# Attention, then a squared-ReLU MLP, on one core: the last norms spread over units, one batch's split operands spread over items, and another order of the second product

## The chip, the cores and the metric

The kernel runs on one core of one Trainium2 chip (trn2). The metric is the device time of one execution in microseconds (us); the time before is the median of three runs. The engines are called PE (TensorE, matmuls), DVE (VectorE), ACT (ScalarE), POOL (GpSimd) and SP (SyncE, which issues the DMAs).

## The reference

Shapes: batch B = 4, heads H = 8, sequence S = 576, head dimension D = 64; the MLP has 2304 tokens, model width 512 and inner width 2048.

```python
scores = q @ k.T / sqrt(D)
x = (log1p(|i - j|) / log1p(max(i, 1)))[..., None]
scores = scores + (relu(x @ w1 + b1) @ w2).transpose(2, 0, 1)[None]
attn = exp(scores - max(scores)); attn = attn / (sum(attn) + 1e-9)
x = (attn @ v).transpose(0, 2, 1, 3).reshape(B * S, H * D)
out = relu(x @ w_in) ** 2 @ w_out
```

## The kernel before, in words

**Attention.** The work is a list of units `(b, hp, ic)`: batch, pair of heads, and one of five chunks of 128 query rows (the fifth, `ic == TAIL`, has 64 rows of both heads). The first NA = 40 units belong to batches 0 and 1 and run chunk by chunk, so that the bias table can be built beside them; the others belong to batches 2 and 3 and run pair of heads by pair of heads. A unit u has on PE: the scores (`score_products`, L429, into `sp`, four PSUM banks), two units later the transposes of the exponentials (`transposes`, L509 into banks a and b as `pp`, L512 into bank c as `pa`), and three units later the product with v (`values`, L528, bank d as `px`). TL = 2 is that distance. DVE adds the bias and finds the row maximum (L439), ACT takes the exponential (L444), which also sums the rows, and copies the transposes to SBUF (L778 in phase one, L963 in phase two).

**Norms.** When a pair of heads has all its chunks, its sums are inverted (`norm_inverse`, DVE, L454), split into three bf16 parts (`norm_parts`, POOL, L460), turned round by one matmul (`norm_rows`, L467, tile `rp`), copied by ACT (`norm_copy`, L472, tile `rows`), spread over the partitions by ten small matmuls (`spread_rows`, L489, tiles `ra` and `rt` in banks a and b), and multiplied into the result `xT` by DVE (`times_rows`, L495). In phase two, `norm_job` queues these steps as stages of a job. Each stage names its engine, a cost and, as the last entry, the first unit in which it may run.

**Order in phase two.** In each step s of the loop at L949 the program writes the order out: scores of s, transposes of s - 2, then for each of two halves ACT's copies and the exponential, between them the values of s - 3 and `fill(s, 0)`; then `fill(s, 1)` and `fill(s, 2)`. `fill(s, slot)` goes through the waiting jobs and issues each first stage whose slot this is, whose unit has come and for whose engine there is room. `SLOT` puts PE and ROW stages into slot 0, LAST (the multiplies) into 2 and all others into 1; `lag` says whether the next stage of a job may run in the same step. Before, `rp` of a norm stands in slot 0 of step u + 3 at the end of PE's unit, its copy `rows` right behind it, and the spreading in slot 0 of step u + 4. Units 37, 38 and 39 are those of phase one whose norms fall into phase two.

**MLP.** The weights and x are split into a high and a low part, and the first product uses seven products of sums and differences of blocks in place of eight. 40 items `(n, P)` (n: 512 tokens of batch n, or for n = B the four rests of 64; P: one of eight pairs of inner blocks) are processed in the order of `runs`; items 0 to 3 are of batch 0, items 4 to 7 of batch 1. Iteration i of the loop at L1135 has on PE the first products of item i (`products`, L1027, into `ha` and `hb`, 24 and 18 matmuls) and then the second product of item i - 1 (`down`, L1119, into four banks y0 to y3, 24 matmuls, or 12 for n = B). Between them other engines do, in program order: the parts `gh` (ACT, L1063) and `gl` (DVE, L1064) of item i - 1; `lead` of raw weight tiles (ACT L186, DVE L188 to L192), ACT's copy of their high part (L644) and POOL's low part (L650); the combinations `c` of item i (ACT L1041, DVE L1043 to L1046); `sums_x`, `high_x`, `low_x` (POOL L719, ACT L725, DVE L732), which make the seven operands m = 1 to 7 of a later batch at the items in `split_at`; and the squared ReLU of item i (ACT L1052 and L1053 for the first 32 items). `leave` takes finished banks y to SBUF (ACT copies, or DVE adds at L1089 where part of the sum was stored before) and issues the DMA.

The second product was, for each half f of the item and each bank k:

```python
for m, (a, x) in enumerate(((gh, wh), (gh, wl), (gl, wh))):
    PE.matmul(y_t[n][k], lhsT=a[:, slot, o:o + 128], rhs=x, ...)
```

The PSUM banks a to d of the attention become y0 to y3 of the MLP, in the order in which the y tiles are first made.

Of the kernel before, what the change touches and what calls it, by code (L numbers as in the profile page):

```python
# [68 lines left out]
TL = 2  # L69
# [8 lines left out]
def attention_then_relu2_mlp(ctx: ExitStack, tc: tile.TileContext, q, k, v, cols, w_in, w_out, psi, xmat, dist, out):  # L78
# [378 lines left out]
    def norm_parts(s):  # L457
        parts = att.tile([128, 3, 9], BF16, name="parts", tag="parts", bufs=2)
        for n in range(3):
            POOL.tensor_copy(out=parts[:, n], in_=s)  # L460
            if n < 2:
                POOL.tensor_tensor(out=s, in0=s, in1=parts[:, n], op=ALU.subtract)
        return parts

    def norm_rows(parts, tag=None):
        rp = bank("rp", tag)[:27, :128]
        PE.matmul(rp, lhsT=parts.rearrange("p n c -> p (n c)"), rhs=ident_b, start=True, stop=True)  # L467
        return rp

    def norm_copy(rp):  # L470
        rows_t = att.tile([27, 128], BF16, name="rows", tag="rows", bufs=2)
        ACT.copy(rows_t, rp)  # L472
        return rows_t
# [162 lines left out]
    def lead(n, upto=7):  # L636
        if upto & 1:
            scratch[n] = stage_p["p"].tile([128, 2, 256], F32, name="wa", tag="wa", bufs=3)
        lead_w(n, scratch[n].bitcast(I32), upto)
# [70 lines left out]
    def halves(n, m):  # L710
        one, op, two = RIGHT[m]
        for cs, *half in x_pieces(n):
            yield cs, op, half[one[1]][:, 2 * one[0]:2 * one[0] + 2], half[two[1]][:, 2 * two[0]:2 * two[0] + 2] if op else None

    def sums_x(n, ms):
        for m in ms:
            for cs, op, a, b in halves(n, m):
                if op:
                    POOL.tensor_tensor(out=sum_at[m][:, :, cs], in0=a, in1=b, op=op)  # L719

    def high_x(n, ms):
        for m in ms:
            hi = split_to[n % 2][m][0]
            for cs, op, a, b in halves(n, m):
                ACT.activation(out=hi[:, :, cs], in_=sum_at[m][:, :, cs] if op else a, func=AF.Identity, scale=xsig[n])  # L725

    def low_x(n, ms):
        w = width[n]
        for m in ms:
            hi, lo = split_to[n % 2][m]  # L730
            for cs, op, a, b in halves(n, m):
                DVE.scalar_tensor_tensor(out=lo[:, :, cs], in0=sum_at[m][:, :, cs] if op else a, scalar=xsig[n], in1=hi[:, :, cs], op0=ALU.mult, op1=ALU.subtract)  # L732
            xs_t[n, m] = (hi[:, :, :w], lo[:, :, :w])

    def store_x(n):
# [63 lines left out]
    room = {}  # L799

    def lag(a, b):
        return int(a != b and a != "PE" and (a, b) != ("DVE", "POOL"))

    SLOT = {"PE": 0, "ROW": 0, "LAST": 2}

    def job(at, *stages):
        jobs.append([at, list(stages)])
# [18 lines left out]
    def norm_job(u):  # L826
        b, hp, ic = units[u]
        st = {"s": sum_t.pop((b, hp))}
        job(
            u + 1,  # L830
            ("DVE", 0.4, lambda: norm_inverse(st["s"])),
            ("POOL", 1.3, lambda: st.update(parts=norm_parts(st["s"])), u + TL),
            ("PE", 0, lambda: st.update(rp=norm_rows(st["parts"], "a")), u + TL + 1),
            ("ROW", 0.24, lambda: st.update(rows=norm_copy(st["rp"]))),
            ("PE", 0, lambda: st.update(r=spread_rows(st["rows"], ("a", "b"))), u + TL + 2),
            ("LAST", 0.9, lambda: times_rows(b, hp, *st["r"])),
        )
        jobs.insert(len(norms), jobs.pop())
        norms.append(jobs[len(norms)])
# [103 lines left out]
    with tc.manual_schedule():  # L943
        job(NA + 1, *(("DVE", 0.68, lambda k=k: scan(k)) for k in range(NF)))
        x_job(NA + 4, 0)
        x_job(NA + 7, 1)
        for u in range(NA - TL - 1, NA):
            norm_job(u)
        for s in range(NA, NU + TL + 2):  # L949
            now[0] = s  # L950
            full = s < NU and units[s][2] < TAIL
            room["DVE"] = min(room.get("DVE", 0), 0.3) + (1.65 if full else 2.5)
            room["ACT"] = min(room.get("ACT", 0) + (0.45 if full else 1.9), 1.5)
            loads(s)
            if s == NA:
                for m, tag in enumerate(raws):
                    fetch_in(ins[m], tag)
            if s < NU:
                negm, sps = score_products(s, False)
            copies = transposes(s - TL, ("a", "b", "c")) if s - TL < NU else []  # L960
            for n in range(2):
                for c in copies[n:n + 1 if n == 0 else None]:
                    ACT.copy(*c)  # L963
                if n:
                    px = values(s - TL - 1, "d") if s - TL - 1 < NU else None
                    fill(s, 0)
                if s < NU and n < len(sps):
                    softmax(s, n, negm, sps[n])
            while waiting:
                b, hp, rows_t = waiting.pop(0)  # L970
                times_rows(b, hp, *spread_rows(rows_t, ("a", "b")))
            if s < NU and ends(s):
                norm_job(s)
            fill(s, 1)
            fill(s, 2)
            if px:
                keep_values(s - TL - 1, *px)
# [19 lines left out]
    lead_at = {1: (6, 7), 2: (10, 11), 3: (14,), 4: (15,)}  # L997
    lead_at.update({5: (16,), 9: (17,), 12: (20,), 13: (21,), 14: (18, 19), 15: (22, 23)})
    lead_at.update(zip(range(18, 26), ((n,) for n in range(24, 32))))
    split_at = {0: (1, (2, 5, 3, 4)), 3: (1, (1, 6, 7))}  # L1000
    split_at.update({i + j: (n, ms) for i, n in ((6, 2), (10, 3), (30, B)) for j, ms in enumerate(((2, 5, 3, 4), (1, 6, 7)))})
    largest_at = {4: 2, 8: 3, 28: B}
    raw_outs = [18, 19, 22, 23, 26, 27, 30, 31]
# [27 lines left out]
    def sums(i, ha, hb):  # L1031
        n, P = items[i]
        w = width[n]
        alpha = alpha_t[n]
        if i % 2:
            c, s = (take(1, o, 1024).rearrange("p (m t) -> p m t", m=4)[:, :, :w] for o in (4480, 5504))
        elif i < NP // 2:
            c, s = (tmp_p.tile([128, 4, 256], F32, name=x, tag=x) for x in "cs")
        else:
            c, s = (xT[1][:, :, 256 * x:256 * x + w] for x in range(2))  # L1040
        ACT.activation(out=s, in_=ha[:, :, :w], func=AF.Identity, scale=alpha)  # L1041
        stt = DVE.scalar_tensor_tensor
        stt(out=c[:, 2:4], in0=ha[:, 1:3, :w], scalar=alpha, in1=s[:, 0:4:3], op0=ALU.mult, op1=ALU.subtract)  # L1043
        stt(out=c[:, 0:2], in0=ha[:, 2:4, :w], scalar=alpha, in1=s[:, 0:2], op0=ALU.mult, op1=ALU.add)
        stt(out=c[:, 2:4], in0=hb[:, 0:1, :w].to_broadcast([128, 2, w]), scalar=alpha, in1=c[:, 2:4], op0=ALU.mult, op1=ALU.add)  # L1045
        stt(out=c[:, 2:4], in0=hb[:, 1:3, :w], scalar=alpha, in1=c[:, 2:4], op0=ALU.mult, op1=ALU.add)  # L1046
        c_t[i] = c

    def squares(i):
        c = c_t[i]  # L1050
# [6 lines left out]
    def parts_g(i):  # L1057
        c, w = c_t[i], width[items[i][0]]
        for f in range(2):
            gh = mlp.tile([128, 2, 256], F32R, name="gh", tag="gh", bufs=2)[:, :, :w]  # L1060
            gl = mlp.tile([128, 2, 256], F32R, name="gl", tag="gl", bufs=2)[:, :, :w]
            g = c[:, 1 - f:4:2]
            ACT.copy(gh, g)  # L1063
            DVE.tensor_tensor(out=gl, in0=g, in1=gh.bitcast(F32), op=ALU.subtract)  # L1064
            g_t[i, f] = (gh, gl)
# [38 lines left out]
    def down(i):  # L1104
        n, P = items[i]
        w = width[n]
        nk = w // 64
        if (n, P) in firsts:
            y_t[n] = [py_p.tile([128, 512], F32, name=f"y{k}") for k in range(nk)]
        order = [(f, k) for f in range(2) for k in range(nk)]  # L1110
        if i == NI - 1:
            order.sort(key=lambda x: x[1])
        for f, k in order:
            wh, wl = w_t[4 * P + 2 + f]
            gh, gl = g_t[i, f]
            t, o = divmod(128 * k, w)
            slot = t if f else 1 - t
            for m, (a, x) in enumerate(((gh, wh), (gh, wl), (gl, wh))):
                PE.matmul(  # L1119
                    y_t[n][k], lhsT=a[:, slot, o:o + 128], rhs=x,  # L1120
                    start=((n, P) in firsts and f == 0 and m == 0), stop=((n, P) in lasts and f == 1 and m == 2),
                )
            if (n, P) in lasts and f == 1:
                leave(n, P, k)
        if (n, P) in lasts and P < NP - 1:
            for j in range(2):
                part_y[n, j] = ready_y[j, "dram"]

    tmp_p = tmp_stack.enter_context(tc.tile_pool(name="tmp", bufs=1, side="right", reuse_waits="tile"))
    with tc.manual_schedule():  # L1130
# [4 lines left out]
        for i in range(NI + 1):  # L1135
# [11 lines left out]
            if i:  # L1147
                parts_g(i - 1)
            one, *two = lead_at.get(i, (None,))
            if one is not None:  # L1150
                lead(one)
            if i < NI:
                sums(i, ha, hb)
# [18 lines left out]
                fetch_out(raw_outs.pop(0))  # L1172
            if i in split_at:
                low_x(*split_at[i])
            if i + 1 in split_at:
                sums_x(*split_at[i + 1])
            if i in largest_at:
# [63 lines left out]
```

## Time and profile before

| what | value |
|---|---|
| median of 3 runs | 747.92 us (747.54 to 748.41) |
| profiled execution, its own time | 748.49 us |
| its span | 746.7 us |
| PE busy | 712.3 us (95%) |
| DVE busy | 556.7 us (75%) |
| ACT busy | 473.8 us (63%) |
| POOL busy | 180.0 us (24%) |
| mean granted clock of PE | 0.971 |

A row of a timeline is one stretch of like instructions of one engine: start, length, line, output<-inputs, shape, count, and in brackets the idle time before it and what ended that. The granted clock (PEclk) is a share of full speed. PE's matmuls overlap a little in these rows, so durations in the prediction are taken from start to start.

### The profile page before, as it was taken

What the parts mean: (1) busy time and instruction counts of PE and PEld (TensorE: products, weight loads), DVE (VectorE), ACT (ScalarE), POOL (GpSimd) and SP (SyncE); (2) the same over time, 40 slices, a digit from 0 to 9 for tenths busy, and PEclk for the clock granted to TensorE, in tenths of its full rate; (3) what the DMA queues carried; (4) which work ended last, traced back from release to release, by engine and by line L of the source; (5) the groups of instructions that cost most, each with busy time, mean ns of one, the idle gap of its engine ahead of it and who ended that gap; (6) DMA issues with size and microseconds to landing.
All of it is one profiled execution on the core that took longest, in us unless ns stands there. A gap on an engine that the chain in (4) does not pass through costs nothing. (4 is left out here: it accounts for less than half of the span.)

```text
span 746.7 us, 18201 instructions
## 1 busy us (share of the span) xinstructions
PE 712.3 (95%) x7382; PEld 576.5 (77%) x7382; DVE 556.7 (75%) x1186; ACT 473.8 (63%) x946; POOL 180.0 (24%) x289
## 2 busy tenths in 40 slices
PE   6889999999989999999998999999999999999992
PEld 6867878787767776777786888888888888888881
DVE  6699888885667889888898878878568775567661
ACT  4367887877756878888756756776476564455220
POOL 1464333332110037432442213112011112001000
PEclk7599999999999999999999999999999999999997
DMA  6630000003437512410442241240038322533100
GB/s 203 192 92 19 3 18 2 2 2 92 174 114 255 185 48 84 136 57 3 142 183 99 109 188 65 105 188 26 1 114 312 124 72 99 212 114 113 57 2 29
DMA packets 31608, 75.34 MB, mean 101 GB/s; under 512 B 5540, under 2 KB 13732, under 8 KB 30500
## 3 DMA queue, kind: packets, MB, share of 16 engines
q1 hardware_dynamic: 31524, 74.17, 28.7%
q8 instruction: 58, 0.95, 0.5%
q14 instruction: 26, 0.21, 0.1%
HBM read 55.81 MB, written 18.35 MB: 99 GB/s over the span
## 5 line engine op out<-in xcount | busy, mean ns | idle before, releaser
L1119 PE MATMUL y<-w,gh 128*128 128x512 f32 x576 | 182.9, 399 | 2.4 <-ACT gh L1063 1.5
L1027 PEld LDWEIGHTS <-area 128*128 128x128 f16 x1680 | 147.6, 98 | 24.8 <-issue 10.1
L439 DVE CUSTOM_DVE_ANT_0 t<-sp,area 128x576 f32<-128x576 f32 x144 | 103.7, 753 | 32.5 <-PE sp L429 29.9
L1119 PEld LDWEIGHTS y<-w,gh 128*128 128x128 f32 x576 | 105.9, 189 | 24.2 <-ACT gh L1063 3.2
L444 ACT ACTIVATE p<-t,negm 128x576 f32<-128x576 f32 x144 | 111.5, 776 | 13.2 <-DVE negm L439 13.0
L1119 PE MATMUL y<-w,gl 128*128 128x512 f32 x288 | 113.8, 395 | 0.7 <-DVE gl L1064 0.7
L429 PE MATMUL sp<-k,q 64*128 64x288 f32 (+1 forms) x640 | 99.6, 426 | 1.6 <-DMA q<-in_q 1.2
L528 PE MATMUL px<-pt,v 128*64 128x128 f32 (+1 forms) x1600 | 97.6, 269 | 2.3 <-DVE bt L384 1.2
L528 PEld LDWEIGHTS px<-pt,v 128*64 128x64 f32 x1600 | 79.9, 138 | 17.7 <-issue 5.9
L1027 PE MATMUL ha<-area 128*128 128x256 f16 (+1 forms) x816 | 85.4, 260 | 0.0
L509 PE MATMUL pp<-ident,p 128*128 128x128 f32 x576 | 83.0, 282 | 0.4 <-DVE xT L495 0.3
L509 PEld LDWEIGHTS pp<-ident,p 128*128 128x128 f32 x576 | 62.1, 141 | 22.7 <-issue 9.3
L389 POOL TENSOR_TENSOR area<-bt,bt 128x256 f32<-128x256 f32 x72 | 53.7, 768 | 73.6 <-DVE bt L384 73.6
L429 PEld LDWEIGHTS sp<-k,q 64*128 64x128 f32 (+1 forms) x640 | 52.7, 175 | 22.6 <-issue 8.0
L367 DVE TENSOR_TENSOR mask<-sdist,theta 128x1024 f16<-128x1024 f16 x81 | 56.1, 728 | 13.8 <-PE bb L397 7.6
L1119 PEld LDWEIGHTS y<-w,gl 128*128 128x128 f32 x288 | 54.4, 189 | 14.1 <-DVE gl L1064 2.0
L1027 PE MATMUL hb<-area 128*128 128x256 f16 (+1 forms) x612 | 64.9, 260 | 0.0
L963 ACT COPY pt<-pp 128x512 f32<-128x512 f32 x76 | 43.8, 577 | 30.0 <-PE pp L509 30.0
L1064 DVE TENSOR_TENSOR gl<-area,gh 128x512 fp32r<-128x512 f32 (+1 forms) x40 | 25.8, 668 | 29.7 <-ACT gh L1063 28.1
L778 ACT COPY pt<-pp 128x512 f32<-128x512 f32 x68 | 37.6, 587 | 14.1 <-PE pp L509 14.0
L650 POOL TENSOR_TENSOR w<-wa,w 128x512 fp32r<-128x512 f32 x16 | 20.8, 1299 | 86.6 <-ACT w L644 86.6
L1064 DVE TENSOR_TENSOR gl<-xT,gh 128x512 fp32r<-128x512 f32 (+1 forms) x36 | 25.6, 749 | 20.8 <-ACT gh L1063 19.2
(161 smaller groups left out, 1042.9 us busy)
## 6 DMA issues: line engine op xcount, KB each, us to landing
raw<-in_w_in SPq DMA_DIRECT2D x32, 512.0 KB, 4.1
r<-in_w_out SPq DMA_DIRECT2D x16, 512.0 KB, 5.0
xs<-area SPq DMA_DIRECT2D x4, 1792.0 KB, 13.3
py<-o SPq DMA_DIRECT2D x12, 512.0 KB, 3.4
o<-py SPq DMA_DIRECT2D x12, 512.0 KB, 4.1
v<-in_v SPq DMA_DIRECT2D x16, 320.0 KB, 4.1
q<-in_q SPq DMA_DIRECT2D x32, 128.0 KB, 3.0
out<-o SPq DMA_DIRECT2D x8, 512.0 KB, 2.9
```

What stands on the lines that cost most here:

```text
L367: DVE.tensor_tensor(out=out, in0=win, in1=th, op=ALU.is_ge)
L389: POOL.tensor_tensor(out=dst, in0=tw, in1=sw, op=ALU.add)
L429: mm = PE.matmul(out_t[to, x, :HALF], lhsT=qt[rows, cols], rhs=kt[rows, k0:k0 + HALF], start=True, stop=True)
L439: DVE.tensor_tensor_reduce(out=t.rearrange("p (x n) -> p x n", x=2), in0=sp[:, :, :HALF], in1=bias.rearrange("p (x n) -> p x n", x=2), sca ...
L444: ACT.activation(out=p[:, S * n:S * n + S], in_=t, func=AF.Exp, bias=negm[:, n:n + 1], scale=-1.0, accum_out=sums[:, 2 * ic + n:2 * ic + n ...
L509: PE.transpose(pp[:, 128 * c:128 * c + 128], p[:, k0:k0 + 128], ident)
L528: PE.matmul(px[64 * h:64 * h + 64, :w], lhsT=vt[:, c, h], rhs=src, start=(c == 0), stop=(c == 4))
L778: ACT.copy(dst, src)
L963: ACT.copy(*c)
L1027: PE.matmul(h[:, s, :w], lhsT=a, rhs=x, start=(k == 0), stop=(k == 5))
L1064: DVE.tensor_tensor(out=gl, in0=g, in1=gh.bitcast(F32), op=ALU.subtract)
L1119: PE.matmul(y_t[n][k], lhsT=a[:, slot, o:o + 128], rhs=x, start=((n, P) in firsts and f == 0 and m == 0), stop=((n, P) in lasts and f == 1 ...
```

## The change

At the boundary one norm goes to each of the steps 42, 43 and 44; in all norms of phase two `rp` moves to a new slot 3 behind the scores, into bank c, with its copy at once. The operands m = 1, 6, 7 of batch 1 are made one per item in items 1, 2 and 3 (all three were made in item 3), their sums in the used scratch tile `s` of the item before; the lead of weight tile 15 moves from item 4 to the end of item 3. The banks of y are made in the order 2, 3, 0, 1, and in each half of `down` all products with gh come ahead of those with gl.

```diff
+    def sum_of(n, m):
+        return sum_at.get((n, m), sum_at.get(m))
...
-                    POOL.tensor_tensor(out=sum_at[m][:, :, cs], in0=a, in1=b, op=op)
+                    POOL.tensor_tensor(out=sum_of(n, m)[:, :, cs], in0=a, in1=b, op=op)
...
     def lag(a, b):
-        return int(a != b and a != "PE" and (a, b) != ("DVE", "POOL"))
+        return int(a != b and a not in ("PE", "ROW") and (a, b) != ("DVE", "POOL"))
 
-    SLOT = {"PE": 0, "ROW": 0, "LAST": 2}
+    SLOT = {"PE": 0, "ROW": 3, "LAST": 2}
...
             ("DVE", 0.4, lambda: norm_inverse(st["s"])),
-            ("POOL", 1.3, lambda: st.update(parts=norm_parts(st["s"])), u + TL),
-            ("PE", 0, lambda: st.update(rp=norm_rows(st["parts"], "a")), u + TL + 1),
-            ("ROW", 0.24, lambda: st.update(rows=norm_copy(st["rp"]))),
-            ("PE", 0, lambda: st.update(r=spread_rows(st["rows"], ("a", "b"))), u + TL + 2),
+            ("POOL", 1.3, lambda: st.update(parts=norm_parts(st["s"])), u + TL + (u < NA)),
+            ("ROW", 0.24, lambda: st.update(rows=norm_copy(norm_rows(st["parts"], "c"))), u + TL + 2 + (u < NA)),
+            ("PE", 0, lambda: st.update(r=spread_rows(st["rows"], ("a", "b"))), u + TL + 2 + (u < NA)),
             ("LAST", 0.9, lambda: times_rows(b, hp, *st["r"])),
...
                 negm, sps = score_products(s, False)
+            fill(s, 3)
             copies = transposes(s - TL, ("a", "b", "c")) if s - TL < NU else []
...
-    split_at = {0: (1, (2, 5, 3, 4)), 3: (1, (1, 6, 7))}
+    split_at = {0: (1, (2, 5, 3, 4)), 1: (1, (1,)), 2: (1, (6,)), 3: (1, (7,))}
+    ahead = {3: 15}
...
         c_t[i] = c
+        if i + 1 in split_at and i < NP // 2 - 1:
+            n, (m,) = split_at[i + 1]
+            sum_at[n, m] = s[:, 0:2]
...
+            gl = mlp.tile([128, 2, 256], F32R, name="gl", tag="gl", bufs=2)[:, :, :w]
             gh = mlp.tile([128, 2, 256], F32R, name="gh", tag="gh", bufs=2)[:, :, :w]
-            gl = mlp.tile([128, 2, 256], F32R, name="gl", tag="gl", bufs=2)[:, :, :w]
...
-            y_t[n] = [py_p.tile([128, 512], F32, name=f"y{k}") for k in range(nk)]
-        order = [(f, k) for f in range(2) for k in range(nk)]
+            banks = {k: py_p.tile([128, 512], F32, name=f"y{k}") for k in (2, 3, 0, 1) if k < nk}
+            y_t[n] = [banks[k] for k in range(nk)]
+        order = [(f, k, m) for f in range(2) for ms in ((0, 1), (2,)) for k in range(nk) for m in ms]
...
-            if one is not None:
+            if one is not None and one not in ahead.values():
                 lead(one)
...
                 low_x(*split_at[i])
+            if i in ahead:
+                lead(ahead[i])
             if i + 1 in split_at:
                 sums_x(*split_at[i + 1])
```

## Rows read from the trace of the kernel before

**Rows 1.** The page, busy us (share of the span) and instructions, PE alone.

```profile
PE 712.3 (95%) x7382; PEld 576.5 (77%) x7382; DVE 556.7 (75%) x1186; ACT 473.8 (63%) x946; POOL 180.0 (24%) x289
```

**Rows 2.** The chain of waits: start us, us, what; two stretches of the second product.

```profile
395.67 6.79 PE y L1119 x22
...
427.59 5.48 PE y L1119 x24
```

**Rows 3.** Stretches of 2 us: busy us (instructions) of the engines, PEclk, DMA share, GB/s.

```profile
222.00:224.00 2.00, 2.00 (x15) 1.67 (x15) 1.51 (x5) 1.71 (x4) 0.00 (x0) 0.50 0.00 0
396.00:398.00 2.00, 2.00 (x6) 1.52 (x6) 1.90 (x5) 0.32 (x1) 0.00 (x0) 0.50 0.00 0
```

**Rows 4.** Timeline of PE at the boundary, start us, us, line, tiles [idle before].

```profile
213.85 0.22 PE L467 MATMUL rp<-ident_b,parts 128*27 128x128 bf16 x1 [0.56 <-POOL sums L462]
...
215.16 1.10 PE L509 MATMUL pp<-ident,p 128*128 128x128 f32 x8
...
217.54 0.41 PE L489 MATMUL ra<-rows,pick 27*64 27x128 bf16 x8
...
218.73 0.41 PE L489 MATMUL ra<-rows,pick 27*64 27x128 bf16 x8 [0.73 <-DVE xT L495]
...
219.92 0.22 PE L467 MATMUL rp<-ident_b,parts 128*27 128x128 bf16 x1 [0.75 <-DVE xT L495]
...
221.24 1.87 PE L509 MATMUL pp<-ident,p 128*128 128x128 f32 x8
...
225.23 0.41 PE L489 MATMUL ra<-rows,pick 27*64 27x128 bf16 x8
```

**Rows 5.** Tile rt, 230 to 360 us, idle before its instructions until (us, times).

```profile
  ACT pt L963: 1.5, 4
```

**Rows 6.** Timeline of PE at the start of the MLP.

```profile
371.79 0.70 PE L1119 MATMUL y<-w,gh 128*128 128x512 f32 x2 [0.85 <-DVE xT L495]
...
377.66 2.79 PE L1027 MATMUL ha<-area 128*128 128x256 f16 x24
...
382.18 0.71 PE L1119 MATMUL y<-w,gh 128*128 128x512 f32 x2
...
394.29 0.73 PE L1119 MATMUL y<-w,gh 128*128 128x512 f32 x2 [1.54 <-ACT gh L1063]
395.67 0.80 PE L1119 MATMUL y<-w,gl 128*128 128x512 f32 x1 [0.65 <-DVE gl L1064]
...
402.30 2.79 PE L1027 MATMUL ha<-area 128*128 128x256 f16 x24
```

**Rows 7.** Timeline of DVE at the start of the MLP.

```profile
377.91 0.42 DVE L188 TENSOR_SCALAR wa<-wa 128x512 f32<-128x512 f32 x1
...
381.44 1.95 DVE L1064 TENSOR_TENSOR gl<-area,gh 128x512 fp32r<-128x512 f32 x2 [1.20 <-ACT gh L1063]
...
385.57 0.74 DVE L1043 SCALAR_TENSOR_TENSOR c<-ha,small,s 128x512 f32<-128x512 f32 x1
...
388.33 0.92 DVE L188 TENSOR_SCALAR wa<-wa 128x512 f32<-128x512 f32 x1
...
401.15 0.74 DVE L732 SCALAR_TENSOR_TENSOR area<-area,small 128x512 f16<-128x512 f32 x1
```

**Rows 8.** Timeline of POOL at the start of the MLP.

```profile
376.00 1.30 POOL L650 TENSOR_TENSOR w<-wa,w 128x512 fp32r<-128x512 f32 x1 [10.54 <-ACT w L644]
...
387.68 1.29 POOL L719 TENSOR_TENSOR area<-xT 128x512 f32<-128x512 f32 x1
```

**Rows 9.** Timeline of ACT at the start of the MLP.

```profile
380.27 0.62 ACT L644 CAST w<-wa 128x512 fp32r<-128x512 f32 x1
380.80 1.13 ACT L1063 CAST gh<-area 128x512 fp32r<-128x512 f32 x2
...
399.08 0.72 ACT L725 ACTIVATE area<-area,small 128x512 f16<-128x512 f32 x1
```

**Rows 10.** Timeline of DVE at the end of a later run of items.

```profile
572.72 2.73 DVE L1089 TENSOR_TENSOR o<-o,y 128x512 f32<-128x512 f32 x4 [1.36 <-PE y L1119]
```

More of the change, by code (lines that the diff above doesn't have):

```diff
@@ L724, in high_x @@
             for cs, op, a, b in halves(n, m):
-                ACT.activation(out=hi[:, :, cs], in_=sum_at[m][:, :, cs] if op else a, func=AF.Identity, scale=xsig[n])
+                ACT.activation(out=hi[:, :, cs], in_=sum_of(n, m)[:, :, cs] if op else a, func=AF.Identity, scale=xsig[n])
     def low_x(n, ms):
@@ L731, in low_x @@
             for cs, op, a, b in halves(n, m):
-                DVE.scalar_tensor_tensor(out=lo[:, :, cs], in0=sum_at[m][:, :, cs] if op else a, scalar=xsig[n], in1=hi[:, :, cs], op0=ALU.mult, op1=ALU.subtract)
+                DVE.scalar_tensor_tensor(out=lo[:, :, cs], in0=sum_of(n, m)[:, :, cs] if op else a, scalar=xsig[n], in1=hi[:, :, cs], op0=ALU.mult, op1=ALU.subtract)
             xs_t[n, m] = (hi[:, :, :w], lo[:, :, :w])
@@ L1108, in down @@
         if (n, P) in firsts:
-            y_t[n] = [py_p.tile([128, 512], F32, name=f"y{k}") for k in range(nk)]
-        order = [(f, k) for f in range(2) for k in range(nk)]
+            banks = {k: py_p.tile([128, 512], F32, name=f"y{k}") for k in (2, 3, 0, 1) if k < nk}
+            y_t[n] = [banks[k] for k in range(nk)]
+        order = [(f, k, m) for f in range(2) for ms in ((0, 1), (2,)) for k in range(nk) for m in ms]
         if i == NI - 1:
             order.sort(key=lambda x: x[1])
-        for f, k in order:
+        for f, k, m in order:
             wh, wl = w_t[4 * P + 2 + f]
@@ L1117, in down @@
             slot = t if f else 1 - t
[L1118 to L1123, printed above, removed]
+            PE.matmul(
+                y_t[n][k], lhsT=(gl if m == 2 else gh)[:, slot, o:o + 128], rhs=wl if m == 1 else wh,
+                start=((n, P) in firsts and f == 0 and m == 0), stop=((n, P) in lasts and f == 1 and m == 2),
+            )
+            if (n, P) in lasts and f == 1 and m == 2:
                 leave(n, P, k)
```

## The prediction, made before the change was run

> **What bounds the kernel now.** I read the page's busy times first: TensorE (PE) works 712.3 us of a span of 746.7 [rows 1]. Only PE's 34 us of idle time, and time in which its clock is low, can be won; no matmul is added or removed here. The chain of waits comes second: from 395.67 us to the end it is PE matmuls almost alone, 24 matmuls of the second product in 5.48 us per item [rows 2]. Nothing in items 3 to 39 is late, so this change can win time only before that point. Third come the granted clocks: two stretches in mid-kernel stand at 0.50, the lower of TensorE's two levels (1.2 of 2.4 GHz) [rows 3]. Then I read PE's timeline just ahead of both, and there the waits are that this change touches: three at the boundary between the attention's two phases [rows 4] and three at the start of the MLP [rows 6]. Both low-clock stretches follow them.
>
> **Part 1, the last three norms of phase one (units 37 to 39).** Each norm is one transpose `rp`, ACT's copy `rows`, ten small matmuls `ra` and `rt`, and two multiplies on DVE. Before, 37 and 38 share a unit and 39 is right behind, all through bank a: `rp` of 38 waits 0.56 us (POOL has not finished its parts), the second `ra` waits 0.73 for DVE's multiplies of the first, and `rp` of 39 waits 0.75 for those of the second [rows 4]. After, each has a unit to itself (42, 43, 44), `rp` goes to bank c behind the scores, and its rows are copied while PE transposes. The same matmuls remain, and the waits go: 0.56 + 0.73 + 0.75 = 2.04 us.
>
> Behind these waits the clock falls. From `pp` to `ra` a unit takes 217.54 - 215.16 = 2.38 us at the full clock and 225.23 - 221.24 = 3.99 in the low stretch [rows 3, 4]: 1.61 us more. With PE fed I expect no fall. The bound on the other side is that it falls all the same, worth 0. Part 1: 3.65 us, between 2.04 and 3.65.
>
> POOL's parts of 38 and 39 move one unit later and still come two units ahead of their `rp`. The multiplies of 38 and 39 reach DVE later, but nothing reads those rows of xT before the maxima some units on. If that cover failed, a DVE instruction would wait, at most for one norm's work. No DMA belongs to a norm.
>
> **Part 2, the eight norms of phase two.** `rp` moves from the end of one unit to behind the scores of the next; spreading stays where it was. PE's work is the same. What is queued behind the moved copy on ACT is the unit's first copy of transposes, and on PE `pa`, which uses bank c and so now waits for `rows`. `pa` comes eight transposes after `rp`, a row of 1.10 us [rows 4] that ends a little after `pa` starts, so the copy has about 0.9 us before it is late; where ACT has fill work it will be late by some tenths. In exchange `rt`, which now waits for ACT's copy four times, 1.5 us in all [rows 5], starts later relative to ACT and waits less. The trace has no such wait on bank c. The nearest row is that 1.5 us: I take 0, with 1.0 either way.
>
> **Part 3, the start of the MLP.** Three edits act on one piece. PE's times now [rows 6]: the second product of item 0, y(0), starts at 371.79 after 0.85 us, because y0 lies in bank a, which the last norm's DVE multiply still reads. It takes 377.66 - 371.79 = 5.87 us, the first products of item 2 382.18 - 377.66 = 4.52. y(2) waits 1.54 us for gh, 0.65 for gl, and then runs at the low clock: 402.30 - 394.29 - 0.65 - 5.87 = 1.48 us too long.
>
> Why gh(2) is late is on DVE and POOL. DVE's lead of one weight tile (L188 to L192) is four instructions; unhindered, from L188 at 377.91 to ACT's copy w at 380.27 it is 2.36 us [rows 7, 9]. In item 2 POOL makes three sums L719, 1.29 us the first [rows 8], and L188 takes 0.92 in place of 0.42 [rows 7]: DVE's instruction stands until POOL's has ended. Copy w and gh queue behind that lead on ACT.
>
> After, there is one POOL sum in each of items 0, 1 and 2:
> - Rotated banks: y(0) starts at 371.79 - 0.85 = 370.94; PE is ready for y(1) at 370.94 + 5.87 + 4.52 = 381.33.
> - Item 1 gets a sum behind POOL's L650, which ends at 376.00 + 1.30 = 377.30. It runs to 378.59, so the L188 of 377.91 starts 0.68 late. gh(1), now ready half-way through the pair at 380.80 + 0.57 = 381.37 [rows 9], is ready at 382.05. PE waits 0.72.
> - y(1) and the products of item 3 end at 382.05 + 5.87 + 4.52 = 392.44.
> - All of DVE's item 2 is 0.68 late, so POOL's one sum runs to 387.68 + 0.68 + 1.29 = 389.65, where L188 starts. Copy w comes 2.36 us later, at 392.01, gh(2) 380.80 + 0.57 - 380.27 = 1.10 after that, at 393.11. PE waits 0.67. y(2) ends at 393.11 + 5.87 = 398.98, at the full clock.
>
> Against 402.30 that is 3.3 us. gl no longer counts: eight gh products (8/24 of 5.87 = 1.96 us) stand ahead of the first gl product. If POOL's sums stall nothing, PE is ready at 370.94 + 2 x (5.87 + 4.52) = 391.72 for y(2) and it ends at 397.59: 4.7 us. If the clock still falls, 3.3 - 1.5 = 1.8.
>
> What is added is hidden as follows. Each new high part (0.72 on ACT [rows 9]) stands where ACT waits for DVE's combinations. Each low part (0.74 [rows 7]) stands in the 1.20 us in which DVE waits for gh. Without that cover each would put its own time on gh, 1.5 us together. The lead of w15 moves to item 3 (2.36 on DVE): with two leads, four combinations of 0.74, a low part and gl of at most 1.95, DVE's item is 4.72 + 2.96 + 0.74 + 1.95 = 10.4 us beside PE's 10.4. That is level, and the reserve of items 4 and later, with no lead of w15 left in them, takes what spills; should it not, some tenths.
>
> **Part 4, order of y products in the other items.** The number of matmuls is the same, and I cost the new order at nothing. At a run's end all four banks now finish together. DVE's four adds take 2.73 us [rows 10] and are covered by the next item's first products (4.52); already now three of them queue up behind the squares. Output DMAs leave SP about a microsecond later; what they feed is an item or more away. The last item is sorted by bank as before, so the drain does not change.
>
> A rule speaks against this order. The Trainium skill, "TensorE: Matmul & The Clock Gate", section "A second HAM failure mode: psum-queue depth-cycling", tells of a kernel whose cycling through PSUM banks let the clock swing between its levels. By that rule the sum would come out slower, as the first rival has it; the trace disagrees so far, since the present order changes bank after every third matmul and holds 5.48 us per 24.
>
> **Sum.** 3.65 + 0 + 3.3 = 6.95 us. The profiled execution took 748.49 us, 0.57 more than the median of 747.92. 748.49 - 6.95 = 741.54; less 0.57, **741.0 us** as a median.
>
> **Rivals.**
> - *The new order slows the y products (5%, slower).* The place is all y products, where a bank follows another with each gl matmul. For it: y(0) took 5.87 us where later items take 5.48 [rows 2, 6], so the rate is not fixed. Against: the steady rate holds across bank changes now. Price: (5.87 - 5.48)/24 = 16 ns on each of 864 matmuls (32 items of 24, 8 of 12), 14 us: 741.0 + 14 = 755. It decides from 6.95/864 = 8 ns a matmul.
> - *The clock still falls at one of the two places (17%).* Two new waits of 0.7 remain in the MLP's start, and `pa` may wait at the boundary. A fall costs 1.5 or 1.6 us back: 742.5.
> - *The waits of the MLP's start only move (9%).* gh(1) becomes as late as gh(2) was, by stalls of the leads that I have underrated. Only part 1 is left: 748.49 - 3.65 - 0.57 = 744.3.
> - *The edits do not reach the order on the engines (4%).* Item 0's products already run between the attention's last matmuls, so the program's order is merged by a scheduler, and the three norms could stay bunched. Then about 747.9.
> - *POOL's sums stall nothing (part of the forecast).* 4.7 in place of 3.3: 739.6.
>
> **How the numbers follow.** The forecast with its last variant has 65%, the rivals 5, 17, 9 and 4. Range: down to 739.6 less most of part 2's 1.0, so 738.8; up to 744.3, which takes in the second and third rival. A measurement of this kernel tells some 0.2% (1.5 us) from no change: faster 0.91, within 0.04, slower 0.05.
>
> **What would show it.** Right: no wait over 0.3 us on `rp` and `ra` at 213 to 220 us; a granted clock of 1.00 through both stretches; y(0) directly behind `rt`; y(1) and y(2) waiting 0.7 each for gh, none for gl; then 24 y matmuls in 5.48 us. Wrong: 24 in more than 5.6; a low clock behind 380; `pa` waiting for ACT's rows in most of the eight norms.

## The result, and the profile after

The changed kernel takes 740.69 us (median of 4 runs, 739.99 to 741.05) against 748.16 before (4 runs, the three named above and one more): a ratio of 0.9899, 95% interval 0.9882 to 0.9915. The prediction was 741.0, in a range of 738.8 to 744.3.

PE's busy time on the page fell by 3.6 us of the span's 7.5, though the matmuls are the same, since matmuls at the low clock count as busy for longer (against [rows 1]):

```profile
span 739.2 us, 18203 instructions
PE 708.7 (96%) x7382; PEld 573.4 (78%) x7382; DVE 552.8 (75%) x1186; ACT 472.0 (64%) x946; POOL 180.3 (24%) x289
```

PE's timeline at the boundary, where [rows 4] had three waits: each norm has a unit of its own, and no row has a wait.

```profile
214.48 0.23 PE L467 MATMUL rp<-ident_b,parts 128*27 128x128 bf16 x1
...
217.02 0.41 PE L489 MATMUL ra<-rows,pick 27*64 27x128 bf16 x8
...
218.58 0.23 PE L467 MATMUL rp<-ident_b,parts 128*27 128x128 bf16 x1
...
221.12 0.41 PE L489 MATMUL ra<-rows,pick 27*64 27x128 bf16 x8
...
222.63 0.23 PE L467 MATMUL rp<-ident_b,parts 128*27 128x128 bf16 x1
...
225.16 0.41 PE L489 MATMUL ra<-rows,pick 27*64 27x128 bf16 x8
```

The two places at which the clock stood at 0.50 before [rows 3] now show 1.00: the one at 222 us, and the one behind the start of y(2), which lay at 396 us and lies at 391:

```profile
222.00:224.00 2.00, 2.00 (x18) 1.27 (x16) 1.73 (x6) 0.97 (x4) 0.00 (x0) 1.00 0.75 282
...
391.00:393.00 2.00, 2.00 (x10) 1.66 (x9) 1.90 (x4) 0.06 (x1) 0.00 (x0) 1.00 0.00 0
```

PE's timeline at the start of the MLP, against [rows 6]. y(0) stands directly behind the last norm's `rt` (366.91), and y(1) and y(2) wait for gh, neither for gl:

```profile
366.91 0.19 PE L489 MATMUL rt<-rows,pick 27*64 27x64 bf16 x2
367.03 2.13 PE L1126 MATMUL y<-w,gh 128*128 128x512 f32 x8
...
372.76 2.79 PE L1031 MATMUL ha<-area 128*128 128x256 f16 x24
...
378.10 2.14 PE L1126 MATMUL y<-w,gh 128*128 128x512 f32 x8 [0.58 <-ACT gh L1070]
...
383.71 2.79 PE L1031 MATMUL ha<-area 128*128 128x256 f16 x24
...
389.01 2.11 PE L1126 MATMUL y<-w,gh 128*128 128x512 f32 x8 [0.54 <-ACT gh L1070]
...
394.59 2.79 PE L1031 MATMUL ha<-area 128*128 128x256 f16 x24
```

DVE and POOL at the same place, against [rows 7, 8]. The first L188 stands until POOL's one sum (L722) has ended at 374.67; the next instruction, L189, runs at its own 0.43:

```profile
374.07 0.89 DVE L188 TENSOR_SCALAR wa<-wa 128x512 f32<-128x512 f32 x1
374.99 0.43 DVE L189 TENSOR_SCALAR wa<-wa 128x512 int32<-128x512 int32 x1
...
384.97 0.91 DVE L188 TENSOR_SCALAR wa<-wa 128x512 f32<-128x512 f32 x1
```
```profile
372.16 1.29 POOL L650 TENSOR_TENSOR w<-wa,w 128x512 fp32r<-128x512 f32 x1 [9.30 <-ACT w L644]
373.40 1.27 POOL L722 TENSOR_TENSOR area<-xT 128x512 f32<-128x512 f32 x1
```

For all that follows I cut each profiled span at four rows of PE: the scores of step 41; the first transposes of step 46, behind the three norms; the last norm's `ra`; and the first products of item 5. The second column is thus the boundary, and the fourth the start of the MLP. Everything is in us, from start to start:

| kernel | to step 41 | to step 46 | to last `ra` | to item 5 | to the end |
|---|---|---|---|---|---|
| before | 209.51 | 24.30 | 136.69 | 41.92 | 334.28 |
| changed | 209.76 | 20.57 | 136.33 | 38.25 | 334.29 |
| 1 norms only | 209.42 | 20.57 | 136.56 | 41.88 | 334.27 |
| 2 MLP only | 210.66 | 24.27 | 136.26 | 38.25 | 334.26 |
| 3 norm a unit | 209.32 | 22.13 | 136.26 | 41.92 | 334.27 |
| 4 behind scores | 210.17 | 22.06 | 140.29 | 41.91 | 334.27 |
| 5 old order | 210.47 | 20.60 | 136.50 | 39.01 | 334.22 |
| 6 old banks | 209.66 | 20.57 | 136.49 | 38.28 | 334.30 |
| 7 old split | 209.77 | 20.57 | 136.49 | 41.89 | 334.28 |
| 8 early sums | 209.12 | 20.57 | 136.53 | 37.29 | 334.29 |
| 9 sums twice | 210.17 | 20.57 | 136.53 | 40.17 | 334.26 |
| 10 room shift | 208.48 | 22.08 | 136.51 | 42.00 | 334.23 |
| 11 early, old banks | 210.82 | 20.61 | 136.53 | 37.30 | 334.34 |
| 12 early again | 211.55 | 20.57 | 136.52 | 37.31 | 334.25 |

The stretch to step 41, which no edit here means to touch, varies by 3 us from profile to profile; the others repeat within 0.1 to 0.4 us. So a part worth 1 us shows in the columns and not in a median. From before to changed the boundary gave 3.73 us, the MLP's start 3.67, the stretch between them 0.36, and the tail nothing.

### The profile page after: what moved, and what is told of

It reads as the page before. It is cut to its first block, busy times and chain, and to the rows that moved or that the text cites. A ratio compares the mean times of both kernels' runs of the same rounds, so it can differ in the third digit from the quotient of the medians.

```text
span 739.2 us, 18203 instructions
## 1 busy us (share of the span) xinstructions
PE 708.7 (96%) x7382; PEld 573.4 (78%) x7382; DVE 552.8 (75%) x1186; ACT 472.0 (64%) x946; POOL 180.3 (24%) x289
## 4 chain that ended last, share of the span: by engine, by line
PE 86%; DVE 8%; issue 2%; ACT 2%; DMA 0%; SPq 0%; ACTq 0%; DVEq 0%
PE y L1126 25%; PE ha L1031 12%; PE px L528 11%; PE sp L429 11%; PE hb L1031 9%; PE pp L509 9%; PE bb L378 4%; PE bb L397 2%; DVE mask L367 2%; PE pa L512 1%; DVE t L439 1%; ACT p L444 1%; PE ra L489 1%; ACT pt L966 1%; DVE bt L384 1%
## 5 line engine op out<-in xcount | busy, mean ns | idle before, releaser
L1126 PE MATMUL y<-w,gh 128*128 128x512 f32 x576 | 149.1, 398 | 1.1 <-ACT gh L1070 1.1
L1126 PE MATMUL y<-w,gl 128*128 128x512 f32 x288 | 79.0, 390 | 0.0
L378 PEld LDWEIGHTS <-mask 128*128 128x128 f16 x1152 | 36.9, 100 | 5.4 <-issue 3.9
```

Of the source, the lines that this page charges most:

```text
L378: PE.matmul(bb[:, 64 * (7 - r):64 * (8 - r)], lhsT=m[:, r], rhs=wmov[:, n], start=(n == 0), stop=(n == 1))
L1126: PE.matmul(y_t[n][k], lhsT=(gl if m == 2 else gh)[:, slot, o:o + 128], rhs=wl if m == 1 else wh, start=((n, P) in firsts and f == 0 and m ...
```

## The experiments

**1 and 2: each half alone.** Experiment 1 is the kernel before with the diff's lines on `lag`, `SLOT`, the norm job and `fill(s, 3)`; experiment 2 is the changed kernel with these lines as before.

> The kernel before with the norms' part of the change alone (one norm a step at the boundary, rp behind the scores in bank c). Theory: the boundary gives its 3.65 us (2.04 of waits, 1.61 of clock) and the eight later norms 0 to 0.3, the MLP's start keeps its waits and its low clock: 4.0 us faster than before, about 744.2. Rival (the stretches depend on each other: fed earlier, the MLP's start waits that much longer): under 1 us faster.

> The changed kernel with the norms as before (rp at the end of PE's unit in bank a, bunched at the boundary). Theory: the MLP's part alone gives 3.3 to 3.9 us, about 744.5, with the three waits and the low clock at 213 to 225 us unchanged; with the first experiment it adds up to the whole 7.5. Rival: the parts overlap, and this alone gives nearly all or nearly nothing.

Measured: 745.25 us, ratio 0.9955 (0.994 to 0.9971), and 744.12, ratio 0.9947 (0.9929 to 0.9965): by these ratios 3.4 and 4.0 us of 748.65. The columns say it more sharply: each half changes its own stretch by the same amount as in the whole, and leaves the other's alone (3.73 and 0.04; 0.03 and 3.67). They add up, and the rivals of both expectations fall.

One thing in experiment 1 I had not expected: the MLP's stretch keeps its length (41.88) although its clock does not fall. The first two rows below repeat the waits of [rows 6]; the clock stays at 1.00 behind them, where it was 0.50 before; and the time so saved is lost one item later, in y(3), in a wait for the low part of weight tile 15, which POOL's L650 makes:

```profile
390.33 0.73 PE L1119 MATMUL y<-w,gh 128*128 128x512 f32 x2 [1.54 <-ACT gh L1063]
391.71 0.50 PE L1119 MATMUL y<-w,gl 128*128 128x512 f32 x1 [0.65 <-DVE gl L1064]
...
405.80 0.50 PE L1119 MATMUL y<-w,gh 128*128 128x512 f32 x1 [0.85 <-POOL w L650]
```
```profile
392.00:394.00 2.00, 2.00 (x10) 1.62 (x10) 1.90 (x5) 0.37 (x1) 0.00 (x0) 1.00 0.00 0
```

From the products of item 3 to those of item 4 it has 12.80 us and before 14.31; from there to item 5, 11.60 and before 10.12. The kernel before (first two rows) has POOL's low part of tile 15 at 409.72, just as PE comes to the half of y(3) that reads it; in experiment 1 (last two rows) PE is there by 404.45 and POOL ends at 405.74. The low clock was covering a wait of the same size.

```profile
408.43 1.29 POOL L650 TENSOR_TENSOR w<-wa,w 128x512 fp32r<-128x512 f32 x1 [7.88 <-ACT w L644]
409.67 0.62 PE L1119 MATMUL y<-w,gh 128*128 128x512 f32 x2
...
404.45 0.50 PE L1119 MATMUL y<-w,gh 128*128 128x512 f32 x1
404.47 1.27 POOL L650 TENSOR_TENSOR w<-wa,w 128x512 fp32r<-128x512 f32 x1 [7.88 <-ACT w L644]
```

**3 and 4: which half of the norms' edit.** Experiment 3 takes the step's delay without the new place, experiment 4 the new place without the delay:

```diff
-            ("PE", 0, lambda: st.update(rp=norm_rows(st["parts"], "a")), u + TL + 1),
+            ("PE", 0, lambda: st.update(rp=norm_rows(st["parts"], "a")), u + TL + 1 + (u < NA)),
...
-            ("ROW", 0.24, lambda: st.update(rows=norm_copy(norm_rows(st["parts"], "c"))), u + TL + 2 + (u < NA)),
+            ("ROW", 0.24, lambda: st.update(rows=norm_copy(norm_rows(st["parts"], "c"))), u + TL + 2),
```

(The stages for POOL and the spreading go with these; the first pair is against the kernel before, the second against experiment 1.)

> The kernel before with one norm a step at the boundary, but rp still at the end of the unit in bank a. Theory: rp of the next norm still stands behind the spreading of the last in bank a and waits about 0.75 us for DVE's multiplies, twice, now in separate units; only 0.5 of 2.04 us of waits goes, and the clock holds (1.6): 2.1 us faster, 746.0. Rival (the bunching alone was the cost): 3.65 us faster. Rival (the clock falls behind the two waits that are left): 0.5 us.

> The kernel before with rp behind the scores in bank c, but POOL's parts and rp of norms 37 to 39 one step earlier than in the changed kernel (as the steps' own rules give it). Theory: rp of 37 comes before POOL has its parts and waits about 1.5 us in step 41, the others do not wait: 4.0 less 1.5, some 2.5 us faster, 745.7, and 1.6 less if the clock falls behind it. Rival (the step's delay is not needed): as the first experiment, 4.0 us.

Experiment 3 measured 746.39 us, ratio 0.9975 (0.9962 to 0.9988); its boundary is 24.30 - 22.13 = 2.17 us shorter, as expected. Two waits of 0.72 us on `rp` for DVE's multiplies are left and the clock holds. So the delay is worth the clock and a little (0.6 us of waits), the new place the rest.

```profile
217.77 0.22 PE L467 MATMUL rp<-ident_b,parts 128*27 128x128 bf16 x1 [0.72 <-DVE xT L495]
...
222.65 0.22 PE L467 MATMUL rp<-ident_b,parts 128*27 128x128 bf16 x1 [0.72 <-DVE xT L495]
```

Experiment 4 missed: 751.07 us, ratio 1.0037 (1.0019 to 1.0055), slower than before. Its boundary is as expected (22.06; `rp` of 37 waits 1.48 us for POOL's parts, and the clock holds). The loss is in the next stretch, 140.29. DVE's and PE's timelines there, and the clock:

```profile
240.24 0.69 DVE L195 TENSOR_REDUCE small<-raw 128x1 f32<-128x512 f32 x1 [2.62 <-DMA raw<-in_w_in]
241.52 0.69 DVE L195 TENSOR_REDUCE small<-raw 128x1 f32<-128x512 f32 x1 [0.59 <-DMA raw<-in_w_in]
```
```profile
242.39 1.93 PE L528 MATMUL px<-pt,v 128*64 128x128 f32 x20 [2.65 <-DVE xT L536]
```
```profile
244.00:246.00 2.00, 2.00 (x20) 1.14 (x18) 1.30 (x4) 1.31 (x4) 0.00 (x0) 0.50 0.47 186
```

DVE stands at a scan (L195, its reduction of one raw weight tile) until that tile's DMA has landed, the copy of `px` is queued behind it, PE waits for bank d, and the clock falls to 0.50. The norms' multiplies reserve DVE's `room`, the time that `fill` still has for DVE in a step. So an earlier norm moves the scans, and with them the DMAs, since the program issues the next tile's DMA behind each scan.

**10: that reading, tested.** Experiment 4 with one line that shifts DVE's room so that the scans fall as in the changed kernel:

```diff
+            room["DVE"] += {NA + 1: 0.9, NA + 4: -0.9}.get(s, 0)
```

> The fourth experiment (norms one step earlier, 751.1 us) with DVE's room raised by 0.9 in step 41 and lowered by 0.9 in step 44, so that the scans of raw weights fall into the same steps as in the changed kernel. Theory: what made the fourth slower was DVE standing 2.6 and 0.6 us in two scans for a raw weight tile's DMA, since the earlier norms had pushed four scans into one step; with the scans spread as in the changed kernel these waits and the low clock behind them go, and only the 1.5 us for POOL's parts is left: 745.7. Rival (the rp ahead of its parts made it slower, by what follows that wait): 750 or more.

Measured: 746.92 us, ratio 0.998 (0.9968 to 0.9991). The stretch is 136.51 again, the scans stand in groups as in the changed kernel, none waits for a DMA, and the boundary keeps the wait that was the only one meant to be left:

```profile
PE rp L467 <- POOL parts L460: 1.5, 1, 1.5
```

**5, 6 and 7: the MLP's edits undone,** in the changed kernel: 5 the order, 6 the banks, 7 the split together with the lead of tile 15 (and the sums in their old places):

```diff
-        order = [(f, k, m) for f in range(2) for ms in ((0, 1), (2,)) for k in range(nk) for m in ms]
+        order = [(f, k, m) for f in range(2) for k in range(nk) for m in range(3)]
...
-            banks = {k: py_p.tile([128, 512], F32, name=f"y{k}") for k in (2, 3, 0, 1) if k < nk}
+            banks = {k: py_p.tile([128, 512], F32, name=f"y{k}") for k in range(nk)}
...
-    split_at = {0: (1, (2, 5, 3, 4)), 1: (1, (1,)), 2: (1, (6,)), 3: (1, (7,))}
-    ahead = {3: 15}
+    split_at = {0: (1, (2, 5, 3, 4)), 3: (1, (1, 6, 7))}
+    ahead = {}
```

> The changed kernel with the second product in the old order (bank by bank: gh, gh, gl). Theory: gl of items 1 and 2, which POOL's low part of a weight tile delays, is then wanted by the third matmul and not by the ninth, so y(1) and y(2) wait 0.9 us each for it: 1.3 to 1.8 us slower than the changed kernel, about 742.3, or 744 if the clock falls behind these waits; 24 y matmuls take 5.48 us in later items in both orders. Rival (the order sets the rate of the y products): 24 matmuls take another time, 0.2 us or more an item, 8 us in all, either way. Rival (gl was never late): no change.

> The changed kernel with the banks of y in the old order. Theory: y(0) waits about 0.85 us again for DVE's multiply of the last norm, but y(1) and y(2) wait for gh anyway (0.58 and 0.54 us now) and take it up: within 0.3 us of the changed kernel, 740.7 to 741.0. Rival (PE sets the pace there): the whole 0.85 us comes back, 741.5.

> The changed kernel with batch 1's operands 1, 6 and 7 all made in item 3 again, their sums at the end of item 2, and the lead of weight tile 15 in item 4. Theory: three POOL sums stall the lead of item 2, gh(2) comes 1.4 us later than in the changed kernel, y(2) waits some 2.5 us, y(1) not at all, and the clock falls behind it (1.5): 2.9 us slower, 743.6; 742.1 if the clock holds. Rival (the new order of the y products already removed what hurt): within 0.5 us of the changed kernel.

The old order: 742.52 us, ratio 0.9921 (0.9907 to 0.9936). Its stretch is 39.01, 0.76 longer than the changed kernel's, about half of what I expected (1.3 to 1.8); PE waits for gl in y(0), y(1) and y(2), and no longer for gh:

```profile
PE y L1126 <- DVE gl L1071: 1.9, 3, 0.8
```

The tail is 334.22 us, as in every other kernel: the order does not set the rate, and the rival that said so falls.

The old banks: 741.78 us, ratio 0.9913 (0.9899 to 0.9927), stretch 38.28 against 38.25: nothing, as expected.

The old split: 744.6 us, ratio 0.995 (0.9937 to 0.9963), stretch 41.89. That is the whole gain of the MLP's half: with the new order and the new banks but the old split and the old lead, the stretch is as long as before. So the three edits do not add up: the order is worth 0.76 us beside the new split and nothing beside the old. y(2) waits for gh and the clock falls; y(3) waits for tile 15 as in experiment 1. No run separates the split from the lead of tile 15.

```profile
390.61 3.55 PE L1123 MATMUL y<-w,gh 128*128 128x512 f32 x8 [2.49 <-ACT gh L1067]
...
406.09 1.88 PE L1123 MATMUL y<-w,gh 128*128 128x512 f32 x7 [0.55 <-POOL w L650]
```
```profile
392.00:394.00 2.00, 2.00 (x7) 1.54 (x6) 1.93 (x4) 0.66 (x1) 0.00 (x0) 0.50 0.00 0
```

**8 and 9: POOL's sums taken away from the leads, and doubled.** In experiment 8 all three are made at the end of item 0, into the places that the kernel before used; in experiment 9 each of items 0 to 2 is made twice.

```diff
-            if i + 1 in split_at:
+            if i == 0:
+                sums_x(1, (1, 6, 7))
+            elif i >= NP // 2 and i + 1 in split_at:
                 sums_x(*split_at[i + 1])
```

> The changed kernel with POOL's three sums for batch 1 all made at the end of item 0, where DVE has no lead to do, in the places that the kernel before used. Theory: the L188 of items 1 and 2 then take 0.42 us in place of 0.9, gh(1) and gh(2) come in time, and the waits of 0.58 and 0.54 us go: 1.1 us faster than the changed kernel, 739.6. Rival (something else makes gh late, ACT's queue or the start of DVE's work behind the last norm): no change.

> The changed kernel with each of POOL's sums for batch 1 of items 0 to 2 made twice in a row. Theory: DVE's lead in items 1 and 2 stands until the second sum has ended too, some 0.85 us more (1.28 of POOL less the 0.42 of the L188 that fits between), so gh(1) is 0.85 and gh(2) 1.7 us later: y(2) starts 1.7 us later, and if the clock falls behind these waits 1.5 more: 1.7 to 3.2 us slower than the changed kernel, 742.4 to 743.9. Rival (DVE's slow L188 has another cause): no change.

Sums twice: 743.92 us, ratio 0.9943 (0.9931 to 0.9956), stretch 40.17, 1.92 us longer. L188 stands for the first sum and L189 for the second, in both items, so the rival falls. PE's waits grow from 0.58 and 0.54 to 1.53 and 1.52 without a fall of the clock:

```profile
374.67 0.90 DVE L188 TENSOR_SCALAR wa<-wa 128x512 f32<-128x512 f32 x1
375.60 1.38 DVE L189 TENSOR_SCALAR wa<-wa 128x512 int32<-128x512 int32 x1
```
```profile
379.66 2.11 PE L1126 MATMUL y<-w,gh 128*128 128x512 f32 x8 [1.53 <-ACT gh L1070]
...
391.54 2.11 PE L1126 MATMUL y<-w,gh 128*128 128x512 f32 x8 [1.52 <-ACT gh L1070]
```

Early sums: 740.54 us, ratio 0.9897 (0.9884 to 0.991). L188 takes 0.42 us in both items, the two waits for gh no longer stand among PE's waits, and the stretch is 37.29, 0.96 us shorter. The median does not show it.

```profile
373.63 0.42 DVE L188 TENSOR_SCALAR wa<-wa 128x512 f32<-128x512 f32 x1
...
384.05 0.42 DVE L188 TENSOR_SCALAR wa<-wa 128x512 f32<-128x512 f32 x1
```

**11 and 12: banks where PE is less late.** Experiment 11 is experiment 8 with the old banks, experiment 12 is experiment 8 again.

> The eighth experiment (sums at the end of item 0; PE waits for nothing from y(0) on) with the banks of y in the old order. Theory: what was worth nothing beside a late gh is worth its whole 0.85 to 0.9 us where PE sets the pace: 0.9 us slower than the eighth kernel. Rival (the wait for the bank is taken up by a later one as in the sixth): under 0.3 us.

> The eighth kernel again, beside the ones it is compared with. Theory: PE's time from the last norm's spreading to the first products of item 4 is 27.0 us again (27.9 in the changed kernel), and the median is about 1 us below the changed kernel's 740.7. Rival (the 1 us in its trace was chance): 27.9.

Measured: 740.97 us, ratio 0.9896 (0.988 to 0.9911), and 740.75, ratio 0.9904 (0.989 to 0.9917). The stretches are 37.30 and 37.31. The theory of 11 fell: y(0) again waits 0.84 us for its bank, and all of it is made up by item 5. In 12, from the products of item 2 to y(1) it takes 4.86 us and in 11 4.51; PE was waiting there too, a little, for what DVE and ACT make. So even in experiment 8 PE does not set the pace from y(0) on; DVE's and ACT's chain from the last norm to gh does, as far as these rows tell. Experiment 12 repeats the 1 us of experiment 8 in the stretch, and again not in the median. The medians of 8, 11 and 12, 740.54 to 740.97, lie on both sides of the changed kernel's 740.69, so experiment 8 is shown to beat it in the stretch alone.

## Why the prediction was right, step by step

- *Part 1, 3.65 us:* 3.73, by the two causes named (waits and low clock). Experiment 3 separates them: with 0.60 of the 2.04 us of waits gone its boundary is 2.17 shorter, which leaves 1.57 for the clock (1.61 in the working). That the delay of one step is needed was said only in passing ("two units ahead of their `rp`"): without it `rp` waits 1.48 us.
- *Part 2, 0 within 1.0:* the stretch with old norms is 136.26 to 136.69, with new ones 136.33 to 136.56, experiment 4 aside. `rt` waits once, 0.4 us, in place of 1.5, and `pa` waits once for `rows`, 0.6: the exchange that was forecast. These are the rows of the tiles `rt` and `rows`:

```profile
  ACT pt L966: 0.4, 1
```
```profile
  PE pa L512: 0.6, 1
```

- *Part 3, 3.3 us:* 3.67 in the column, which ends at item 5. At the products of item 4, for which the 3.3 was worked out, it was 3.87: from the last `ra` 402.30 - 370.50 = 31.80 before and 394.59 - 366.66 = 27.93 after. y(3) gave 0.2 back, as tile 15 is still a little late: its 24 matmuls take 5.72 us on the chain of waits and took 5.51 before.

  The terms were less exact than the sum. The waits left were given as 0.72 and 0.67 from start to start; so taken they are 378.10 - 372.76 - 4.52 = 0.82 and 389.01 - 383.71 - 4.52 = 0.78. The rows put only 0.58 and 0.54 of them down as idle, since PE's rows overlap. What made up for this is that y(0), y(1) and y(2) took 5.73, 5.61 and 5.58 us, and not the 5.87 of y(0) before. The stall of L188 is 0.89 - 0.42 = 0.47 us, not 0.68: DVE comes to it 0.67 us behind the sum's start (0.61 in the working), and L188 ends 0.29 behind the sum's end, where the working added its whole 0.42.
- *Part 3, the owner of 1.48 us:* here the working was wrong though the sum was right, and that was luck. It booked the low clock behind y(2) as a loss that goes with its waits, and the move of tile 15's lead at nothing but some tenths of cost; it gave no gain as a reason for that move. Experiment 1 shows the clock held and the time lost all the same to tile 15. That the time is really won takes the earlier lead as well; this is argued, since experiment 7 puts that lead back together with the sums and loses both. An estimate from rows says the same: in experiment 1 the low part of tile 15 was ready 405.74 - 400.14 = 5.60 us behind the start of DVE's gl for y(3). With the old lead the changed kernel, where that gl starts at 398.85, would have it at 404.45, and PE comes to the half of y(3) that reads it at 401.96.

```profile
398.85 1.29 DVE L1071 TENSOR_TENSOR gl<-area,gh 128x512 fp32r<-128x512 f32 x2
...
401.96 2.21 PE L1126 MATMUL y<-w,gh 128*128 128x512 f32 x8
```

- *Banks:* named with 0.85 us in the working and worth nothing in the time (experiments 6 and 11), as gh is late anyway. The sum had that, since it was made on y(1) and y(2).
- *Part 4, nothing:* right. The tail is the same to 0.12 us in all kernels. The rival had its price from unlike terms: 5.87 us of y(0) is from start to start and 5.48 is a length on the chain; from start to start y(3) before took 412.42 - 406.82 = 5.60. The Trainium skill's page "TensorE: Matmul & The Clock Gate" (section "A second HAM failure mode: psum-queue depth-cycling") tells of a kernel in which PE idled for short times between its groups of matmuls as it cycled through banks, and the clock swung. The trace does not show that here: with 16 changes of bank in an item in place of 8, no wait of PE stands from 410 to 725 us, the granted clock is 1.00 there, and 24 matmuls take 5.48 us.

```profile
420.09 5.48 PE y L1126 x24
```

- *Missing in the prediction:* DVE's `room` couples the norms to the scans and so to the DMAs of raw weights. In the changed kernel it did no harm; in experiment 4 it cost 3.8 us (140.29 against 136.51 in experiment 10).

## What to carry to other kernels

Sum a start-up stretch to a point behind its last wait, not to the first wait that goes: what stood behind it (a slow clock, a late bank, a late tile) may already have been hidden by the next one. Where an order comes from a budget, list what else draws on it before moving a step, and look for the DMAs that this will start later. Spread a second engine's work so that one piece at a time stands beside instructions that it can stop, or none does (experiment 8, as far as the stretch shows it).

## What the runs showed of the hardware

- The granted clock did not follow the length of a wait alone. Behind the same two waits (1.5 to 1.6 and 0.65 us) it fell in the kernel before and in experiments 3 and 10, and held in 1 and 4; it held behind 1.53 in experiment 9, and fell behind 2.49 and 2.65 in 7 and 4. At the boundary it fell behind waits of 0.56, 0.73 and 0.75 in the kernel before, and held behind one of 1.48 or 1.49 in 4 and 10 and behind two of 0.72 in 3. What else decides it is not shown.
- DVE's L188 and L189, which read and write SBUF alone, stood until POOL's running sum had ended: 0.89 to 0.92 us for L188 against 0.42 alone, and with a second sum 1.38 for L189 against 0.43. The combinations, which read PSUM, ran beside POOL's L650 at their usual 0.74 to 0.75.
